# The first pair's scores and softmax ahead of the first weight group's conversion

## Chip, core and metric

The kernel runs on one NeuronCore of a Trainium2 chip. The metric is the device time of one execution in microseconds (us). The engines are TensorE (PE for matmuls, PEld for its weight loads), VectorE (DVE), ScalarE (ACT), GpSimd (POOL) and SyncE (SP, which here only issues DMAs).

## What is computed

Three stages run one after the other on 2304 tokens (4 batches of 576), all in float32:

```python
scores = q @ k^T / 8            # 4 batches, 8 heads, 576 tokens, head size 64
attn   = softmax(mask(scores))  # causal by blocks of 64 tokens
x      = attn @ v               # heads side by side: 2304 x 512
x = (sigmoid(x @ w_gate) * (x @ w_val)) @ w_out          # 512 -> 1536 -> 512
p = probs / sum(probs)
out = sum over 4 experts e:  p[:, e] * (relu(x @ w1[e]) @ w2[e])   # 512 -> 1024 -> 512
```

The weights of the middle stage arrive as 64-bit floats and are turned into 32-bit ones on the chip.

## The kernel before

**Precision.** A float32 product is made of three matmuls: each operand is split into a high part and the rest (`split_sb`: ACT or POOL writes the high part, DVE or POOL the rest). Sums of weight blocks and of activations save some of the products.

**Attention.** `attn_items` writes down a queue of steps for all 16 pairs of heads (4 batches of 4 pairs). A pair's scores are cut into tiles of 128 query rows, t = 0 to 4. A step `s_mm` makes a tile's scores on PE (line 350 for batch 0), then DVE masks (380), takes the row maximum (381, or 411 and 413 for the last tile, t4) and ACT the exponential (383, 416). Three steps later `p_tr` transposes the tile on PE (459, 479) and ACT copies it out (446, tiles pTa and pTb). `pv_both` multiplies with v (119, tile obank), makes the inverse sums (491 to 510) and scales (541). `prep_tr` transposes the next pair's q and k (230) with copies on ACT (238). The copies and the exponentials share ACT; the transposes of all steps share two PSUM banks (tbank). `loads` and `load_v` put a pair's DMAs on SP.

**Conversion.** `conv_items(f)` has twelve steps for one of twelve weight groups of the middle stage: `raw(0)` and `raw(1)` issue the two DMAs of 512 KB (647); `f64(0)` and `f64(1)` turn them into float32 (ACT 614, DVE 615 and 616); four `sums` on POOL (662) and four `part` steps split the results (ACT 131, DVE and POOL 129 and 133), and store them in DRAM (670, tile w1d) for later passes. There are three raw buffers, so the fourth raw DMA waits until the first buffer has been read by its last `sums`.

**Order.** Every step of the attention queue has a cost and so a place: its batch, plus the share of the batch's cost that lies ahead of it. `attn_to(A00)` first emits all steps with a place under 0.12 (items 0 to 21 of the queue). The rest of the queue up to place 1.05 (A1[0]) is then merged evenly with the conversion of the first five groups (NC0). After that come the first matmuls of the middle stage (L1: tiles c, weights wa, wb, wc, wd; it begins with group 4, whose parts stay in SBUF) and its inputs (`x1_prep`, tile xc), which need the four pairs of batch 0. Later steps of batches 1 to 3 and the conversion of groups 5 to 11 are mixed into L1.

**What the emitted order means.** It is a priority. The planner (`schedule_with_timeline_sim`) runs its own model of the engines and gives each engine's instructions the order in which they came up there; each engine then works through its list strictly in that order. `pinned(fn)` (102) ties each DVE, ACT and POOL instruction that `fn` emits behind the instruction emitted just before it on the same engine, in order alone, without a semaphore. Before the change only steps of the last middle pass use it (331).

Of the kernel before, what the change touches and what calls it, by code (L numbers as in the profile page):

```python
# [18 lines left out]
NC0 = 5  # L19
FIRST = (4, 0, 5, 1, 6, 2, 7, 3, 8, 9, 10, 11)  # L20
A00 = 0.12
A1 = [1.05, 2.3, 4, 4, 4]
PACE1 = 0.9
GB = 4
# [19 lines left out]
def _merge(a, b, pace=1.0):  # L44

    ta = sum(c for c, _ in a) or 1.0
    tb = sum(c for c, _ in b) or 1.0
    i = j = 0
    ca = cb = 0.0
    while i < len(a) or j < len(b):  # L50
        if j >= len(b) or (i < len(a) and pace * ca / ta <= cb / tb):
            c, fn = a[i]
            i += 1
            ca += c
        else:
            c, fn = b[j]
            j += 1
            cb += c
        fn()
# [3 lines left out]
def attention_moe_moe_kernel(  # L63
# [21 lines left out]
    NF = DFF // P  # L85
# [16 lines left out]
    def pinned(fn):  # L102

        def run_in_order():
            done = nc.cur_bb.bb.instructions
            n = len(done)
            fn()
            for i in range(n, len(done)):
                e = done[i].engine
                if e in (mybir.EngineType.DVE, mybir.EngineType.Activation, mybir.EngineType.Pool):  # L110
                    prev = next((x for x in reversed(done[:i]) if x.engine == e), None)
                    if prev is not None:
                        tc.add_manual_dep(done[i], prev.name, NOSYNC, reason="in the order given")

        return run_in_order
# [8 lines left out]
    def split_sb(hi, lo, src, eng_hi="v", eng_lo="v"):  # L124

        if eng_hi == "v":
            nc.vector.tensor_copy(out=hi, in_=src)
        elif eng_hi == "p":
            nc.gpsimd.tensor_scalar(out=hi, in0=src, scalar1=1.0, scalar2=1.0, op0=ALU.mult, op1=ALU.mult)
        else:  # L130
            nc.scalar.activation(out=hi, in_=src, func=AF.Copy)  # L131
        e = nc.vector if eng_lo == "v" else nc.gpsimd
        e.tensor_tensor(out=lo, in0=src, in1=hi.bitcast(F32), op=ALU.subtract)
# [474 lines left out]
    def from_f64(bits, out=None):  # L608

        lo, hi = bits[:, :, 0], bits[:, :, 1]
        f = lo if out is None else out.bitcast(I32)
        nc.scalar.activation(out=hi.bitcast(F32), in_=hi.bitcast(F32), func=AF.Prelu, scale=2.0 ** -112, alpha=2.0 ** 32)
        nc.vector.tensor_scalar(out=f, in0=lo, scalar1=29, scalar2=None, op0=ALU.logical_shift_right)
        nc.vector.scalar_tensor_tensor(  # L616
            out=f, in0=hi, scalar=3, in1=f, op0=ALU.logical_shift_left, op1=ALU.bitwise_or)
        return f.bitcast(F32)
# [15 lines left out]
    def w1_tile(k):  # L634
        n = 1 if k == "d" else 2
        return moe1.tile([P, 2, n, QF], F32R, tag="wd" if k == "d" else "wg", name=f"w{k}", bufs=2 if k == "d" else 6)

    def w1_at(f, k):
        return wc_d[f][:, WAT[k][0] * QF:WAT[k][1] * QF].rearrange("p (h n f) -> p h n f", h=2, f=QF)

    def conv_items(f):

        d = {}

        def raw(gv):
            t = d["raw", gv] = conv.tile([P, NKT, P, 2], I32, tag="raw", name="raw", bufs=3)
            nc.sync.dma_start(
                out=t.rearrange("p c f t -> p c (f t)"),
                in_=(w_gate, w_val)[gv].bitcast(I32)[:, 2 * f * P:2 * (f + 1) * P].rearrange("(c p) f -> p c f", p=P))

        def f64(gv):
            d[gv] = from_f64(d["raw", gv].rearrange("p c f t -> p (c f) t"))

        def b(k, a):
            return d[a][:, k * QF:(k + 1) * QF]

        def sums(n):
            if n == 0:
                d["t"] = conv.tile([P, 4, QF], F32, tag="wt", name="wt")
            t = d["t"]  # L660
            x, y = [(b(0, 1), b(0, 0)), (b(1, 1), t[:, 0]), (b(1, 1), b(0, 1)), (b(1, 0), t[:, 1])][n]
            nc.gpsimd.tensor_tensor(out=t[:, n], in0=x, in1=y, op=ALU.subtract)

        def part(k):
            t = w1_tile(k)
            src = dict(a=lambda: d[0], b=lambda: d["t"][:, 0:2].rearrange("p n f -> p (n f)"),
                       c=lambda: d["t"][:, 2:4].rearrange("p n f -> p (n f)"), d=lambda: b(1, 1))[k]()
            split_sb(t[:, 0].rearrange("p n f -> p (n f)"), t[:, 1].rearrange("p n f -> p (n f)"), src,
                     "p" if k in "bc" else "a", "v" if k == "a" else "p")
            nc.sync.dma_start(out=w1_at(f, k), in_=t.bitcast(F32))  # L670
            if f >= NC0 - 1:
                wg[f, k] = t

        r = [lambda: raw(0), lambda: raw(1), lambda: f64(0), lambda: f64(1), lambda: sums(0), lambda: part("a"),
             lambda: sums(1), lambda: part("b"), lambda: sums(2), lambda: sums(3), lambda: part("c"), lambda: part("d")]
        return [(1.0, x) for x in r]
# [229 lines left out]
    def run(lst):  # L906
        for _, fn in lst:
            fn()

    if True:  # L910
# [380 lines left out]
        def attn_next():  # L1291
            queue[pos[0]][3]()
            pos[0] += 1
            if pos[0] == len(queue):
                pt2.release()
                attn.release()

        def attn_to(target):
            while pos[0] < len(queue) and place[pos[0]] < target:
                attn_next()  # L1300

        attn_to(A00)
        a0 = [(queue[i][2], attn_next) for i in range(pos[0], len(queue)) if place[i] < A1[0]]
        cs = [conv_items(f) for f in range(NF)]
        _merge(a0, sum(cs[:NC0], []), 1.0)
        x_items = x1_prep(0)
        prev = []
        for p in range(NP1):
            at, total = 0.0, NF * 7 * 6 * C1 + NF * 2 * NKT * 3 * C1
            for f0 in range(0, NF, 2):  # L1310
# [39 lines left out]
                if f0 == NF - 2 and p == 0:  # L1350
                    x_items = x1_prep(p + 1)
                    n = len(items)
# [5 lines left out]
                for c, fn in both:  # L1358
                    attn_to(A1[p] + (A1[p + 1] - A1[p]) * min(1.0, at / total / PACE1))
                    fn()  # L1360
# [11 lines left out]
        for p in range(NPASS):  # L1372
            for q0 in range(0, NQ, 2):
                last = p == NPASS - 1 and q0 == NQ - 2
                items = l1_items(p, q0) + l1_items(p, q0 + 1)
                if (p, q0) == (0, 0):
                    m = len(items) // 2
                    items = [items[m * (c == "B") + "1526743".index(x)] for c, x in
                             ("A1", "A2", "A5", "B1", "A6", "B2", "A7", "B6", "B5", "A4", "B7", "A3", "B4", "B3")]
                side = []  # L1380
# [15 lines left out]
                n = len(items)  # L1396
# [48 lines left out]
```

## Time and profile before

| | |
|---|---|
| median of 3 runs | 1411.94 us (1411.53 to 1413.97) |
| profiled execution | 1413.05 us, span of its instructions 1411.3 us |
| PE busy | 1372.7 us (97% of the span) |
| DVE, ACT, POOL busy | 986.3, 777.6, 481.5 us |
| mean granted TensorE clock | 0.993 of 2.4 GHz |

In the profile's rows a time is in us from the start of the span, a mean in ns. A line of the timeline gives the start, the duration, the engine, the line of the kernel, the operation, the tile written and read, and in brackets how long the engine stood idle before and what ended that.

### The profile page before, as it was taken

The page shows a single profiled execution, that of the slowest core. Times are in us where ns is not written, and L with a number is a line of the kernel's source. Part 1 is how long each engine was busy: PE and PEld are TensorE (multiplying, and loading weights), DVE is VectorE, ACT ScalarE, POOL GpSimd, SP SyncE. Part 2 cuts the span into 40 slices and gives each one's busy share as a digit, 9 for nine tenths or more (in the row PEclk, how much of TensorE's full clock was granted, in tenths as well). Part 3 has the DMA queues.
Part 4 walks back from the last instruction along what each step waited for, and adds up shares of the span by engine and source line. Part 5 has one row for each costly group of instructions (what it writes and reads, how often), then busy time and mean ns, then how long its engine had stood idle before and what let it go on. Part 6 is the DMA issues. An engine that isn't in the chain of part 4 may idle for free.

```text
span 1411.3 us, 26204 instructions
## 1 busy us (share of the span) xinstructions
PE 1372.7 (97%) x9212; PEld 1267.3 (90%) x9212; DVE 986.3 (70%) x2103; ACT 777.6 (55%) x1926; POOL 481.5 (34%) x502
## 2 busy tenths in 40 slices
PE   6899999999999999999999999999999999999998
PEld 3467787889988999999999999989999999999998
DVE  6877689976776445466777666757766787766766
ACT  5888788888876333343445444544444454443442
POOL 4753346301122200022576556533222342322322
PEclk8999999999999999999999999999999999999999
DMA  7999677886657877998799888886666777676754
GB/s 224 299 285 294 214 237 249 267 238 201 194 165 226 298 262 268 319 341 299 273 340 350 298 301 305 288 301 232 232 251 241 258 259 283 245 270 229 275 206 157
DMA packets 210803, 369.57 MB, mean 262 GB/s; under 512 B 74736, under 2 KB 137200, under 8 KB 204528
## 3 DMA queue, kind: packets, MB, share of 16 engines
q1 hardware_dynamic: 209584, 367.62, 77.2%
q8 instruction: 74, 1.21, 0.3%
q14 instruction: 57, 0.47, 0.1%
q10 hardware_dynamic: 1088, 0.26, 0.1%
HBM read 267.82 MB, written 100.01 MB: 261 GB/s over the span
## 4 chain that ended last, share of the span: by engine, by line
PE 86%; DVE 4%; DMA 4%; ACT 3%; issue 1%; SPq 1%; POOL 1%; DVEq 0%; ACTq 0%; POOLq 0%
PE c L119 38%; PE o L119 26%; PE lo L119 7%; PE s L119 4%; PE obank L119 3%; PE t L119 3%; PE tbank L459 2%; DMA raw<-in_moe_w_val_dram 1%; PE s L350 1%; PE tbank L230 1%; PE tbank L479 1%; DVE raw L616 1%; DMA w1g<-w1d 1%; DVE nm L381 0%; ACT pt L383 0%
## 5 line engine op out<-in xcount | busy, mean ns | idle before, releaser
L119 PE MATMUL c<-xc,w1g 128*128 128x384 f32 x1920 | 384.6, 338 | 1.5 <-DMA w1g<-w1d 1.2
L119 PEld LDWEIGHTS c<-xc,w1g 128*128 128x128 f32 x1920 | 330.5, 188 | 7.7 <-DVE hb L1073 1.4
L119 PE MATMUL o<-w2s,hb 128*128 128x256 f32 x1728 | 243.5, 282 | 1.1 <-DVE acc L1222 1.1
L119 PEld LDWEIGHTS o<-w2s,hb 128*128 128x128 f32 x1728 | 231.8, 189 | 2.0 <-DVE acc L1222 1.7
L1222 DVE SCALAR_TENSOR_TENSOR acc<-o,pr_t,acc 128x256 f32<-128x256 f32 x264 | 123.4, 479 | 57.9 <-PE o L119 55.8
L1082 POOL TENSOR_TENSOR hs<-hf 128x384 f32<-128x384 f32 x64 | 64.0, 1022 | 287.5 <-ACT hf L1090 256.4
L119 PE MATMUL lo<-g,wo 128*128 128x288 f32 x888 | 150.8, 301 | 5.0 <-DVE x L895 3.0
L119 PE MATMUL o<-w,hb 128*128 128x512 f32 x576 | 142.8, 391 | 0.0
L119 PEld LDWEIGHTS lo<-g,wo 128*128 128x128 f32 x888 | 126.4, 188 | 11.0 <-DVE x L895 5.1
L1090 ACT ACTIVATE hf<-c 128x384 f32<-128x384 f32 x128 | 65.7, 513 | 115.1 <-DVE c L1127 57.8
L119 PEld LDWEIGHTS o<-w,hb 128*128 128x128 f32 x576 | 107.2, 188 | 18.5 <-DVE acc L1166 0.2
L1127 DVE TENSOR_TENSOR c<-c,snap 128x384 f32<-128x384 f32 x144 | 77.8, 552 | 56.0 <-PE c L119 38.4
L1120 ACT ACTIVATE snap<-c 128x384 f32<-128x384 f32 x144 | 65.7, 484 | 87.1 <-PE c L119 86.8
L1071 ACT ACTIVATE hb<-hs 128x384 fp32r<-128x384 f32 x128 | 63.3, 518 | 64.4 <-POOL hs L1082 64.2
L1073 DVE TENSOR_TENSOR hb<-hs,hb 128x384 fp32r<-128x384 f32 x128 | 87.2, 696 | 5.5 <-ACT hb L1071 5.2
L895 DVE TENSOR_TENSOR x<-lo,x 128x288 f32<-128x288 f32 x124 | 55.7, 453 | 45.7 <-PE lo L119 44.9
L119 PE MATMUL c<-xc,wa 128*128 128x288 f32 x504 | 83.9, 300 | 1.8 <-ACT xc L131 1.6
L383 ACT ACTIVATE pt<-s,nm 128x128 f32<-128x128 f32 (+3 forms) x128 | 67.5, 529 | 17.9 <-DVE nm L381 10.7
L119 PEld LDWEIGHTS c<-xc,wa 128*128 128x128 f32 x504 | 71.8, 189 | 4.2 <-ACT xc L131 2.2
L119 PE MATMUL c<-xc,wc 128*128 128x288 f32 x432 | 70.8, 298 | 0.4 <-ACT snap L819 0.4
L819 ACT ACTIVATE snap<-c 128x288 f32<-128x288 f32 x108 | 44.4, 411 | 41.4 <-PE c L119 41.0
L459 PE MATMUL tbank<-ident,pt 128*128 128x128 f32 x320 | 53.6, 282 | 12.5 <-ACT pTa L446 7.7
(180 smaller groups left out, 2707.1 us busy)
## 6 DMA issues: line engine op xcount, KB each, us to landing
w1g<-w1d SPq DMA_DIRECT2D x96, 512.0 KB, 5.3
w2s<-w2d SPq DMA_DIRECT2D x48, 1024.0 KB, 6.2
w1d<-w1g SPq DMA_DIRECT2D x48, 512.0 KB, 4.9
wa<-w1d SPq DMA_DIRECT2D x40, 512.0 KB, 5.0
wb<-w1d SPq DMA_DIRECT2D x40, 512.0 KB, 5.1
wc<-w1d SPq DMA_DIRECT2D x40, 512.0 KB, 4.3
wo<-wod SPq DMA_DIRECT2D x36, 512.0 KB, 5.8
wr<-in_moe_w_dram SPq DMA_DIRECT2D x32, 512.0 KB, 5.4
```

What stands on the lines that cost most here:

```text
L119: ins = nc.tensor.matmul(out=out, lhsT=lhsT, rhs=rhs, start=start, stop=stop, skip_group_check=skip)
L383: ins = nc.scalar.activation(out=pt[:, x * nk:(x + 1) * nk], in_=sp[:, x - x0], func=AF.Exp, bias=nm[:, j0 + x:j0 + x + 1], scale=1.0, acc ...
L459: nc.tensor.transpose(out=tbank[:, x * P:(x + 1) * P], in_=pt[:, x * P:(x + 1) * P], identity=ident)
L819: nc.scalar.activation(out=t, in_=d["c1"][:, :TH1], func=AF.Copy)
L895: nc.vector.tensor_tensor(out=x2[t, dm], in0=ps, in1=x2[t, dm], op=ALU.add)
L1071: nc.scalar.activation(out=t[:, 0], in_=src, func=AF.Copy if low is None else AF.Relu)
L1073: nc.vector.tensor_tensor(out=t[:, 1], in0=src, in1=t[:, 0].bitcast(F32), op=ALU.subtract)
L1082: nc.gpsimd.tensor_tensor(out=o, in0=x, in1=y, op=op)
L1090: nc.scalar.activation(out=hf[q, blk], in_=c, func=AF.Relu)
L1120: nc.scalar.activation(out=t, in_=d["c1"][:, :TH], func=AF.Copy)
L1127: nc.vector.tensor_tensor(out=c, in0=d[tag][:, :TH], in1=d[n], op=ALU.add)
L1222: nc.vector.scalar_tensor_tensor(out=o, in0=ps, scalar=pr, in1=o, op0=ALU.mult, op1=ALU.add)
```

## The change

```diff
+A01 = 0.25
...
         attn_to(A00)
+        cs = [conv_items(f) for f in range(NF)]
+        run(cs[0][:2])
+        attn_to(A01)
+        cs[0] = [(c, pinned(fn) if n < 2 else fn) for n, (c, fn) in enumerate(cs[0][2:])]
         a0 = [(queue[i][2], attn_next) for i in range(pos[0], len(queue)) if place[i] < A1[0]]
-        cs = [conv_items(f) for f in range(NF)]
         _merge(a0, sum(cs[:NC0], []), 1.0)
```

The two raw DMAs of group 0 are emitted right behind item 21. Then items 22 to 38 of the attention queue follow (places 0.124 to 0.240): all that is left of the first pair's scores and softmax with the transposes of its tiles, its first product with v, the keys of the second pair, the second pair's tiles t0 to t2, and the loads of the third pair. The other ten steps of group 0 come after them. `f64(0)` and `f64(1)` are pinned: their DVE and ACT instructions stand behind the last one emitted there. The 58 conversion steps that remain are merged with the attention steps from place 0.251 to 1.05.

## Rows read from the trace of the kernel before

**Rows 1.** Busy time, share and instructions of each engine.
```profile
PE 1372.7 (97%) x9212; PEld 1267.3 (90%) x9212; DVE 986.3 (70%) x2103; ACT 777.6 (55%) x1926; POOL 481.5 (34%) x502
```

**Rows 2.** Busy us (instructions) by stretch: stretch, length, engines, granted clock, DMA share, GB/s.
```profile
16.90:37.30 20.40, 12.41 (x63) 7.12 (x63) 19.00 (x42) 15.50 (x45) 15.94 (x17) 0.67 0.90 278
37.30:97.00 59.70, 52.04 (x347) 31.03 (x345) 49.35 (x135) 48.09 (x151) 38.23 (x43) 1.00 0.94 291
97.00:160.00 63.00, 62.29 (x436) 48.95 (x437) 47.45 (x120) 54.44 (x161) 25.00 (x26) 1.00 0.81 259
```

**Rows 3.** Timeline of PE around its longest stop.
```profile
16.76 0.38 PE L230 MATMUL tbank<-ident,qn 128*128 128x128 f32 x2
24.03 0.90 PE L459 MATMUL tbank<-ident,pt 128*128 128x128 f32 x3 [6.89 <-ACT pTa L446]
```

**Rows 4.** Timeline of ACT from 14 us to 37 us.
```profile
14.02 0.22 ACT L383 ACTIVATION_READ_ACCUMULATOR pt<-s,nm 128x1 f32 x1
16.93 0.69 ACT L614 ACTIVATE raw<-raw 128x512 f32<-128x512 f32 x1 [2.69 <-DMA raw<-in_moe_w_gate_dram]
...
21.20 0.50 ACT L416 ACTIVATE pt<-s,nm 128x288 f32<-128x288 f32 x1 [0.93 <-DVE nm L413]
...
23.38 0.59 ACT L446 ACTIVATE pTa<-tbank 128x512 f32<-128x512 f32 x1
...
36.68 0.60 ACT L446 ACTIVATE pTb<-tbank 128x512 f32<-128x512 f32 x1
```

**Rows 5.** Timeline of DVE: a wait for raw data, a long step, the second pair's t2.
```profile
16.93 0.43 DVE L615 TENSOR_SCALAR raw<-raw 128x512 int32<-128x512 int32 x1 [3.66 <-DMA raw<-in_moe_w_gate_dram]
17.27 0.45 DVE L411 TENSOR_REDUCE nm<-s 128x1 f32<-128x288 f32 x1
...
27.78 1.49 DVE L615 TENSOR_SCALAR raw<-raw 128x512 int32<-128x512 int32 x1
...
34.75 0.56 DVE L381 TENSOR_REDUCE nm<-s 128x1 f32<-128x384 f32 x1
```

**Rows 6.** Instructions on the raw tiles: busy us by stretch (DVE, ACT, POOL).
```profile
14.30:37.30 23.00, 10.27 (x13) 6.18 (x10) 8.79 (x10) 0.70 0.92 287
```

**Rows 7.** Short stretches: as rows 2.
```profile
8.00:12.00 4.00, 3.73 (x15) 1.94 (x16) 2.39 (x12) 2.20 (x9) 0.00 (x0) 1.00 0.69 155
12.00:14.00 2.00, 2.00 (x11) 0.86 (x9) 1.23 (x4) 1.54 (x5) 0.00 (x0) 1.00 0.94 152
...
17.20:20.00 2.80, 0.00 (x0) 0.00 (x0) 2.74 (x7) 1.81 (x4) 0.12 (x1) 0.88 1.06 209
20.00:22.00 2.00, 0.00 (x0) 0.00 (x0) 1.91 (x4) 1.07 (x4) 2.00 (x3) 0.50 0.99 349
```

**Rows 8.** The raw tiles: ns shortest/median/longest, first and last start.
```profile
L615 DVE TENSOR_SCALAR raw<-raw x36: 412/424/1491, 16.9 to 252.7; 128x512 int32<-128x512 int32 x36
L616 DVE SCALAR_TENSOR_TENSOR raw<-raw x36: 660/692/1659, 17.6 to 253.3; 128x512 int32<-128x512 int32 x36
...
L133 DVE TENSOR_TENSOR wa<-raw,wa x12: 666/683/1466, 19.7 to 239.5; 128x512 fp32r<-128x512 f32 x12
```

**Rows 9.** Timeline of SP's queue: third pair's loads, raw DMAs, group 1's return.
```profile
13.05 1.14 SPq L204 DMA_DIRECT2D qn<-in_q_dram  x2
...
16.40 1.62 SPq L204 DMA_DIRECT2D kn<-in_k_dram  x2
18.07 0.51 SPq L647 DMA_DIRECT2D raw<-in_moe_w_gate_dram  x1
...
104.80 0.32 SPq L681 DMA_DIRECT2D wa<-w1d  x1
```

**Rows 10.** Timeline of POOL: the last conversion step of group 4.
```profile
73.34 1.28 POOL L133 TENSOR_TENSOR wc<-wt,wc 128x512 fp32r<-128x512 f32 x1
```

**Rows 11.** Timeline of DVE: the fourth pair's last scaling.
```profile
89.11 0.49 DVE L541 TENSOR_TENSOR x<-obank,xr 128x320 f32<-128x320 f32 x1 [0.71 <-PE obank L119]
```

**Rows 12.** Timeline of PE: first products with group 4's wc and group 1's wa.
```profile
97.26 1.02 PE L119 MATMUL c<-xc,wc 128*128 128x288 f32 x6 [0.41 <-ACT snap L819]
...
130.64 1.84 PE L119 MATMUL c<-xc,wa 128*128 128x288 f32 x12
```

**Rows 13.** DMA issues between 100 and 140 us: count, KB, us to landing.
```profile
wa<-w1d SPq DMA_DIRECT2D x2, 512.0 KB, 5.9
```

## The prediction

> **What bounds the kernel now.** I read the page's totals first: PE is busy for 97% of the span [rows 1], so a gain has to come from the 38.6 us in which it is not, or from work that PE does slowly. The table of stretches shows where: from 16.9 to 37.3 us PE is busy for 12.41 of 20.40 us at a mean clock of 0.67, from 37.3 to 97 us for 52.04 of 59.70, and from 97 to 160 us for 62.29 of 63.00 [rows 2]. From 97 us on PE itself is the limit. Ahead of it the limit is the feeding of PE: the fourth pair's last scaling comes at 89.11 us [rows 11], and only behind it can the last inputs of L1 be made, while group 4's conversion, which L1 also needs, had its last POOL step at 73.34 us and is first wanted in its late part at 97.26 us [rows 10, 12]. So attention is late and conversion early, by 97.26 - 74.62 = 22.6 us. From 37.3 to 97 us DVE is busy for 83% and ACT for 81% [rows 2]: each is near its limit, and they hand work to each other.
>
> The timelines show what attention loses. PE stops for 6.89 us until 24.03 and waits for the copy pTa [rows 3]. ACT started that copy at 23.38, though the transposes had long been finished: its list puts steps of groups 0 and 1 and the exponentials of tile t4 ahead of it, and those wait for a row maximum [rows 4]. DVE in turn stood for 3.66 us until 16.93 in front of L615, the first step on the raw data, with the maximum of t4 queued behind it [rows 5]. ACT stood 2.69 us at the same data [rows 4].
>
> **The change part by part.** *Moved ahead.* Items 22 to 38 end with the copy of the first pair's last tile, which ACT ended at 36.68 + 0.60 = 37.28 us [rows 4]. ACT's earlier work ends at 14.24 [rows 4]. Between them ACT is busy for 15.50 us [rows 2], 6.18 of them on raw tiles in ten instructions [rows 6]; 9.32 us are attention's. At best ACT runs these without a gap but the 0.93 us for the maximum of t4 [rows 4]: 14.24 + 9.32 + 0.93 = 24.5. At worst it runs them at the share at which attention ran alone from 8 to 14 us, (2.20 + 1.54) / 6.00 = 62% [rows 7]: 14.24 + 15.0 = 29.2. I take the middle, 26.9, since three pair steps overlap here and not two. The lead of attention is then 37.3 - 26.9 = 10.4 us, with ends of 8.1 and 12.8. The stop of 6.89 us goes; what is late next on ACT is the pair of t3 exponentials, and then the tbank copies one behind another.
>
> *Moved behind.* `f64(0)` starts at about 26.9 instead of 16.93, 10 us later (7.6 to 12.3). Its DVE and ACT instructions, two of ACT and four of DVE with those of `f64(1)`, are tied to the end of item 38 on each engine; behind them stand the splits of group 0, and the fourth tiles of the second pair. POOL's steps and the stores are not tied but need these results. The work displaced is 10.27 us of DVE in 13 instructions and 6.18 of ACT in ten [rows 6].
>
> *DMAs.* The raw DMAs of group 0 keep their place. The third pair's loads, which move past group 0's stores, were already issued from 13.05 on, ahead of the third raw DMA at 18.07 [rows 9], so nothing changes in SP's order there; that third DMA has a free buffer and should go at the same time. From the fourth on, raw DMAs and stores follow group 0 by some 10 us. Two slacks cover this. Group 4 would end at 74.62 + 10 = 84.6 and is wanted at 97.26. Group 1's wa comes back by a DMA issued at 104.80 that lands 5.9 us later, and is first used at 130.64 [rows 9, 12, 13]: 19.9 us of slack. I cost the delay of conversion and of DMAs at nothing; if the cover were gone it would cost the part of 10 us beyond these.
>
> *Payback.* What was pushed behind has to be done before or beside pairs two to four. If all of it comes on attention's path, the lead shrinks by DVE's 10.27 us to 10.4 - 10.27 = 0.1. If all of it fits into the 59.70 - 49.35 = 10.35 us in which DVE is idle from 37.3 to 97 [rows 2], the whole 10.4 stays. Since DVE and ACT are over 80% busy there, most idle time is a wait inside a chain that other work can't use; I stay near the first end and take a third of the way: 0.1 + 10.3 / 3 = 3.5 us.
>
> How long is the displaced work really? L615, L616 and the split of wa have medians of 424, 692 and 683 ns, but longest cases of 1491, 1659 and 1466 [rows 8], and one of the long ones ran while POOL converted [rows 5]. At the medians, 5 x 0.424 + 5 x 0.692 + 3 x 0.683 = 7.6 us instead of 10.27. The Trainium skill, "SBUF — State Buffer", section "Who interferes with whom", says that a VectorE instruction with two SBUF inputs, or in a mode using both ports, fully blocks behind a GpSimd instruction; the longest rows agree. By that rule the change removes no blocking, it moves POOL's share of group 0 beside later pairs, and the sum would be the one above; with 7.6 it would be 10.4 - 7.6 + (a third of 7.6) = 5.3.
>
> *PE's clock.* In the stretch without matmuls the granted clock goes from 0.88 to 0.50, 1.2 of 2.4 GHz [rows 7]. The loss lies in the stretch that the first part already replaces, so I add nothing for it. The Trainium skill, "TensorE: Matmul & The Clock Gate", section "What's actually happening", says the throttled state is the default and activity releases it. That speaks against a full gain if PE is only lightly used by attention alone; from 8 to 12 us, where it was, the row shows 1.00 [rows 7].
>
> **Sum.** The profiled execution took 1413.05 us, 1.75 of them around its span of 1411.3. 1413.05 - 3.5 = 1409.5. The median of the runs shown is 1.1 us lower, 1411.94, so the median after is forecast at 1408.4 us, 0.25% faster. L1 would reach its full pace near 93.5 us, and I expect the work behind it, PE being the limit, to follow at the same distance.
>
> **The rivals.**
> *The lead stays nearly whole.* If conversion lags into its 22.6 us of slack and attention keeps running ahead, about 8 of the 10.4 us remain: 1404. For it: DVE and ACT idle time of 10.35 and 11.6 us from 37.3 to 97 [rows 2]. Against it: the merge after item 38 gives each attention step more conversion than before (58 steps in 0.80 of a batch, 1.38% each, against 60 in 0.93, 1.54% each), which spends the lead by design.
> *The lead is spent.* DVE pays back all of its 10.27 us, or the planner's order of the later pairs comes out much as now, because only DVE and ACT of two steps are tied: 0.1 us, 1411.8. For it: DVE is the busiest engine, 19.00 of 20.40 us and then 83% [rows 2].
> *DVE falls behind, slower.* Attention alone takes until 29.2, the lead is 8.1, and the payback 10.27: 2.2 us lost. On top, DVE's tie ends with the second pair's t2, whose last maximum now ends at 35.31 [rows 5], and ACT's with the copy that ends at 37.28 [rows 4]; L616 needs ACT's result, so DVE may stand up to 2.0 us with the maxima of the second pair behind it. Together 2 to 4 us, at 3 in all 1415. It decides from the point where the copy of item 38 ends later than 37.28 - 10.27 = 27.0 us and DVE has no idle time to use.
>
> **How the numbers follow.** This kernel's runs tell 0.2% (2.8 us) from no change. The forecast's own case, 1405 to 1411, has 0.48, of which 0.40 lies below 1409.1; the lead nearly whole 0.13; the lead spent 0.21; DVE behind 0.18. Faster by over 0.2% is 0.40 + 0.13 = 0.53, within 0.2% is 0.08 + 0.21 = 0.29, slower 0.18. The range goes from 1402.5, the lead kept with 1.5 us more of it than in the first rival, to 1415, the middle of the slower case; about 0.15 is left out.
>
> **What would show it.** PE's stop at 17 us gone and the clock at 1.00 from 16.9 to 37.3 us; the first L615 near 27 us instead of 16.93, with no wait for raw data in front; the first pair's last copy near 27; group 4's wc near 84; the fourth pair's last scaling at 85 to 86 instead of 89.11, and PE full from about 93.5. The prediction is wrong if the last scaling is not earlier although the stop is gone (the lead is spent), if DVE is over 90% busy from 27 to 90 us and the scaling is later, or if PE, full from 93.5, loses the time again between 97 and 260 us.

## The result, and the profile after

The changed kernel takes 1422.82 us (median of 6 runs, 1419.98 to 1425.03), the kernel before 1411.74 in the same session (6 runs, 1409.65 to 1413.97): a ratio of 1.0074 with a 95% interval of 1.0063 to 1.0086, so 9 to 12 us slower. The forecast was 1408.4 with a range to 1415; it was wrong in sign and the range missed.

The totals of the profile after answer to [rows 1]: no engine has more to do, only the span is 11.4 us longer (1422.7 against 1411.3). PE idles 49.6 us instead of 38.6.

```profile
PE 1373.1 (97%) x9212; PEld 1264.9 (89%) x9212; DVE 988.7 (69%) x2103; ACT 778.8 (55%) x1926; POOL 482.1 (34%) x502
```

Where PE idles shows in the stretches of the kernel after, in the columns of [rows 2]:

```profile
16.90:37.30 20.40, 13.78 (x75) 7.83 (x77) 8.70 (x30) 11.82 (x38) 0.00 (x0) 0.75 0.29 70
37.30:97.00 59.70, 47.58 (x322) 28.16 (x318) 53.05 (x133) 49.47 (x152) 45.43 (x49) 1.00 0.88 269
97.00:160.00 63.00, 60.45 (x407) 46.35 (x408) 45.16 (x111) 49.85 (x143) 27.17 (x28) 0.97 0.89 298
160.00:300.00 140.00, 130.60 (x923) 111.43 (x924) 124.18 (x298) 114.00 (x312) 63.70 (x60) 1.00 0.80 253
```

and one stretch of the kernel before that stands nowhere yet:

```profile
160.00:300.00 140.00, 134.76 (x963) 116.48 (x961) 121.47 (x305) 117.13 (x323) 53.22 (x53) 1.00 0.78 250
```

PE's busy time falls by 4.46 us from 37.3 to 97, by 1.84 from 97 to 160 and by 4.16 from 160 to 300: 10.5 of the 11.0 us. In the first stretch, where the gain was to arise, PE gains 1.4 us, and it loses as much ahead of it: up to 37.3 us PE is busy for 24.10 us after and 24.08 before. Look in that stretch at the last columns too: DVE does 8.70 us of work instead of 19.00, POOL none instead of 15.94, and the DMA engines are busy for 0.29 of the time instead of 0.90.

PE's stop is still there, and longer, in PE's timeline after (the row that answers to [rows 3]); ACT's, DVE's and SP's say why:

```profile
23.22 0.90 PE L460 MATMUL tbank<-ident,pt 128*128 128x128 f32 x3 [7.81 <-ACT pTa L447]
```
```profile
22.01 0.68 ACT L615 ACTIVATE raw<-raw 128x512 f32<-128x512 f32 x1 [4.70 <-DMA raw<-in_moe_w_gate_dram]
22.59 0.58 ACT L447 ACTIVATE pTa<-tbank 128x512 f32<-128x512 f32 x1
...
34.52 0.60 ACT L447 ACTIVATE pTb<-tbank 128x512 f32<-128x512 f32 x1
...
38.27 0.74 ACT L132 ACTIVATE wa<-raw 128x512 fp32r<-128x512 f32 x1
...
83.65 0.67 ACT L132 ACTIVATE wa<-raw 128x512 fp32r<-128x512 f32 x1
```
```profile
17.72 0.51 SPq L648 DMA_DIRECT2D raw<-in_moe_w_gate_dram  x1
18.32 1.00 SPq L205 DMA_DIRECT2D qn<-in_q_dram  x2
38.03 0.37 SPq L205 DMA_DIRECT2D vh<-in_v_dram  x1
```

Line numbers are one higher than before. The step at 22.01 isn't group 0's, which is tied: it is the first step of group 1, whose raw DMA is issued at 17.72 behind the third pair's loads. Nothing ties it, so the planner put it into the room that group 0 left, ahead of the copy pTa. The first pair's last copy ends at 34.52 + 0.60 = 35.12 us, 2.2 earlier than before [rows 4], not 10.4.

Behind 18.32 SP issues no DMA for 19.7 us. What stands next in its list is the third pair's load of v, which waits for the first pair's product with v; in the kernel before that load comes at 40.51, behind four more raw DMAs and the stores of groups 0 and 1. SP's wait after (us in all, times, longest), and the row before:

```profile
SPq L205 <- PE obank L120: 18.6, 1, 18.6
```
```profile
40.51 0.38 SPq L204 DMA_DIRECT2D vh<-in_v_dram  x1
```

The fourth raw DMA could hardly have gone earlier either: it needs a buffer that POOL's sums set free, and POOL's first sums come at 39.13 us.

What came late is conversion. ACT's copy into wa starts at 38.27 for group 0 and at 83.65 for group 4 (the first and the fifth such row); before, at 18.98 and 63.43:

```profile
18.98 0.65 ACT L131 ACTIVATE wa<-raw 128x512 fp32r<-128x512 f32 x1
...
63.43 0.70 ACT L131 ACTIVATE wa<-raw 128x512 fp32r<-128x512 f32 x1 [1.04 <-DVE raw L616]
```

19.3 us late at group 0 and 20.2 at group 4: nothing is made up. POOL's last step for group 4, at 73.34 before [rows 10], comes at 101.07, 27.7 later. PE's timeline before, then after, shows the price. The first products of L1 take group 4's wa, and before they stand among attention's matmuls:

```profile
73.86 1.03 PE L119 MATMUL c<-xc,wa 128*128 128x288 f32 x6
75.77 1.03 PE L119 MATMUL c<-xc,wa 128*128 128x288 f32 x3
81.16 0.40 PE L119 MATMUL c<-xc,wb 128*128 128x288 f32 x1
```
```profile
86.50 0.81 PE L120 MATMUL c<-xc,wa 128*128 128x288 f32 x4
...
97.27 1.07 PE L120 MATMUL c<-xc,wb 128*128 128x288 f32 x4 [0.75 <-POOL wb L130]
...
103.74 1.03 PE L120 MATMUL c<-xc,wc 128*128 128x288 f32 x6
...
140.61 0.96 PE L120 MATMUL c<-xc,wa 128*128 128x288 f32 x6
```

Group 4's wa is first used 12.6 us later, wb 16.1, wc 6.5, and group 1's wa 10.0 [rows 12]. The matmuls on L1's tile c show what PE loses of L1 from 37.3 to 97 us (before, then after; the columns are PE, PEld, DVE and ACT, clock, DMA share, GB/s):

```profile
37.30:97.00 59.70, 5.48 (x24) 3.53 (x24) 0.46 (x1) 0.68 (x2) 1.00 0.94 291
```
```profile
37.30:97.00 59.70, 2.38 (x12) 1.69 (x12) 0.44 (x1) 0.40 (x1) 1.00 0.88 269
```

Twelve of 24 are gone from there, 3.1 of the 4.46 us. Attention itself is not late: the fourth pair's last scaling is at 87.20 us, 1.9 earlier than [rows 11]:

```profile
87.20 0.49 DVE L542 TENSOR_TENSOR x<-obank,xr 128x320 f32<-128x320 f32 x1
```

### The profile page after: what moved, and what is told of

Read it like the earlier page. It is cut to its first block, busy times and chain, and to the rows that moved or that the text cites. A ratio compares the mean times of both kernels' runs of the same rounds, so it can differ in the third digit from the quotient of the medians.

```text
span 1422.7 us, 26191 instructions
## 1 busy us (share of the span) xinstructions
PE 1373.1 (97%) x9212; PEld 1264.9 (89%) x9212; DVE 988.7 (69%) x2103; ACT 778.8 (55%) x1926; POOL 482.1 (34%) x502
## 4 chain that ended last, share of the span: by engine, by line
PE 81%; DVE 5%; ACT 5%; DMA 5%; issue 2%; POOL 1%; SPq 0%; ACTq 0%; DVEq 0%; POOLq 0%
PE c L120 36%; PE o L120 25%; PE lo L120 6%; PE s L120 4%; PE obank L120 3%; PE t L120 3%; PE tbank L460 2%; PE s L351 1%; ACT pt L384 1%; DMA xr<-xd1b 1%; DVE xc L134 1%; DVE nm L382 1%; PE tbank L231 1%; DMA w1g<-w1d 1%; DMA raw<-in_moe_w_out_dram 1%
## 5 line engine op out<-in xcount | busy, mean ns | idle before, releaser
L120 PE MATMUL lo<-g,wo 128*128 128x288 f32 x888 | 147.7, 299 | 3.5 <-DVE x L896 3.5
L120 PEld LDWEIGHTS o<-w,hb 128*128 128x128 f32 x576 | 107.2, 188 | 18.6 <-DVE acc L1167 0.3
L120 PEld LDWEIGHTS c<-xc,wc 128*128 128x128 f32 x432 | 60.6, 188 | 7.9 <-ACT snap L820 4.7
```

The lines of the kernel that those rows point to most:

```text
L120: ins = nc.tensor.matmul(out=out, lhsT=lhsT, rhs=rhs, start=start, stop=stop, skip_group_check=skip)
```

## The experiments

In each a ratio is to the kernel before, run beside it. The first theory is *late conversion*: L1's first groups come late, and PE loses the L1 work that filled attention's gaps. Its first rival is *the step put ahead*: group 1's raw step and the stop of 7.81 us are the loss. A second one, named any reshuffle or a new order in the expectations, is that whatever order the planner makes anew is worse than the one before. (In the rows of e23 line numbers are two higher than before, in those of the other runs one.)

**e1_pin_next, e2_no_pin.** e1 ties group 1's two steps too; e2 takes the ties out and leaves the order of the program.

```diff
+        cs[1] = [(c, pinned(fn) if n in (2, 3) else fn) for n, (c, fn) in enumerate(cs[1])]   # e1
-        cs[0] = [(c, pinned(fn) if n < 2 else fn) for n, (c, fn) in enumerate(cs[0][2:])]
+        cs[0] = cs[0][2:]                                                                     # e2
```

> The changed kernel with group 1's two f64 steps pinned as group 0's are, so that none of them is put ahead. Late conversion (L1 waits for group 4, whose conversion ended 27.8 us later): PE's stop of 7.8 us goes and the first pair's last copy comes at 27 to 30 us, but group 4's last split still ends at 95 us or later, and the time stays at 1416 to 1423 us. Step put ahead (the stop in front of group 1's raw data is the loss): 1412 us or less.

> The changed kernel without the ties: the raw DMAs and attention steps are emitted early as in the change, and group 0's f64 steps are left to the planner. If the ties alone make the difference: 1412 us, as before, with the first conversion at 16.9 us. If the emitted order does: 1420 us or more.

e1: 1421.68 us, 1.0058 (1.0038 to 1.0078). Its stop is gone (largest wait of PE from 14 to 40 us: 2.45), and attention runs ahead as forecast; ACT's row of the first pair's last copy, and DVE's of the fourth pair's last scaling:

```profile
28.10 0.60 ACT L447 ACTIVATE pTb<-tbank 128x512 f32<-128x512 f32 x1
```
```profile
87.44 0.49 DVE L542 TENSOR_TENSOR x<-obank,xr 128x320 f32<-128x320 f32 x1
```

A lead of 8.6 us at the first, of 1.7 at the second, and still 8 us slower. So the step put ahead falls. e2: 1412.67 us, 0.9998 (0.9989 to 1.0007), and its lists of PE, DVE, ACT and POOL are those of the kernel before, instruction for instruction: the planner undoes the new place of the items, and six tied instructions make all of the difference.

**e3_pins_only, e9_pins_both, e6_a017.** The ties placed earlier: behind item 21 with group 0 alone (e3, without `attn_to(A01)`) or with group 1 too (e9), and at `A01 = 0.17` (e6).

> The ties alone: attention steps emitted ahead only up to item 21 as before the change, group 0's two f64 steps pinned there. Group 1's first step still comes ahead of them and waits for its data until about 22 us, so PE's stop stays, but group 0 converts some 10 us earlier than in the changed kernel. Late conversion: group 4 ends at 80 to 90 us, inside the slack, 1411 to 1415 us. Step put ahead: the stop costs as much as in the changed kernel, 1419 to 1423 us.

> Ties at item 21 for groups 0 and 1: no step waits for raw data ahead of the first pair's softmax, and group 0 converts from about 19 us. Both theories: no stop, conversion late by 2 to 4 us, 1407 to 1412 us. If it is slower than 1414 us, both miss something.

> The changed kernel with the tie a third of the way: items up to place 0.17 of the batch ahead of group 0's conversion instead of 0.25. Late conversion: the conversion chain is delayed by less, group 4's stores near 90 us instead of 102, so 1414 to 1418. The step put ahead: a group's raw data is still waited for ahead of the copies of the transposes, so a stop of 5 us or more near 20 us and 1419 to 1424. Any reshuffle costs: 1419 to 1424 too, but without that stop.

e3: 1429.95, 1.0105 (1.0078 to 1.0133); e9: 1418.61, 1.0038 (1.0026 to 1.0051); e6: 1419.78, 1.0044 (1.0030 to 1.0057). None fitted what late conversion expected. e3 and e9 are slower than any theory said; of e9 the expectation itself said that above 1414 us both miss something. e6 came out as the step put ahead had it, with a stop of 6.59 us and 1419.78, and with group 4 late by 16.8. But in e6 and e3 attention is late, not conversion alone: the fourth pair's last scaling is at 93.44 in e6 and at 100.55 in e3, 89.11 before. In e3 PE waits 6.4 us twice for copies and 4.7 once for DVE. A tie holds up what stands behind it on its engine. e9 is the run that late conversion explains least: group 4's wa copy is 5.4 us late, but its first product is 3.0 us earlier than before.

**e12_before_nc4, e11_after_nc4, e13_pin_nc4.** Four groups converted ahead of L1, group 3 first: the kernel before, the changed one, and e1.

```diff
-NC0 = 5
-FIRST = (4, 0, 5, 1, 6, 2, 7, 3, 8, 9, 10, 11)
+NC0 = 4
+FIRST = (3, 0, 4, 1, 5, 2, 6, 7, 8, 9, 10, 11)
```

> The kernel before with four weight groups converted ahead of L1 instead of five, and group 3 first in L1's order. It is the control of the next two. Late conversion: in the kernel before, conversion is not late, so nothing is gained, 1409 to 1415 us. Any reshuffle costs: the merge of attention and conversion changes from the start, so some 5 to 10 us more, 1417 to 1422.

> The changed kernel with four groups converted ahead of L1 and group 3 first. Group 3's stores come at 87.3 us in the changed kernel, group 4's at 102.4, and L1 wants the first group from about 97. Late conversion: the wait at L1's start goes, 1413 to 1417, at most 4 us above its control e12. The step put ahead (group 1's raw data waited for at 22 us, PE's stop of 7.81 us): the stop is untouched, so about 11 us above the control, 1420 to 1425. Any reshuffle costs: no relation to where L1 starts, 8 to 11 us above the control.

> As e11, with group 1's two steps tied as well (so that PE's stop at 17 to 30 us is gone, as in e1). Late conversion: the stop's 7 us are a gain once L1 no longer waits for a late group: 1405 to 1411, below its control e12. The step put ahead: the stop's going gains what it gained from after to e1, about 1 us below e11. Any reshuffle costs: as e11.

e12: 1421.94, 1.0057 (1.0039 to 1.0075); e11: 1423.16, 1.0067 (1.0052 to 1.0082); e13: 1419.54, 1.0041 (1.0028 to 1.0053). The levels missed, since the control itself lost 8 us. That loss is what the reshuffle theory had expected of it (1417 to 1422), and conversion isn't late in it: its third and fourth copies into wa start at 33.61 and 46.55 us, before at 34.42 and 47.22. The distances, though, are those of late conversion: the change costs 1.2 us here instead of 11, with its stop at 6.15 us, and with the stop gone (e13) it is 2.4 us below its control, where the reshuffle theory had e11 8 to 11 above. (The three intervals overlap.) With one group less before L1, the lateness delays little: the copy into group 3's wa starts at 72.60 in e11 and at 46.55 in e12, and L1's first product comes at 73.47 and 72.84.

**e14_kept, e17_late, e15_kept21, e16_a1.** Is it any new order by the planner that costs, as e12 suggests? In e14, e15 and e17 the order of PE, DVE, ACT and POOL is given, as a list of places in the program:

```diff
+        for a, b in zip(one, one[1:]):
+            tc.add_manual_dep(done[b], done[a].name, dep, reason="in the order given")
```

The list is the planner's for the kernel before, with the shifts that the expectations name. e16 has no list and no tie, but `A1 = [1.1, ...]`.

> The order of the instructions is given for PE, DVE, ACT and POOL: that of the kernel before, with the first pair's steps ahead of group 0's conversion as the change has them, conversion 10 us later at its start, this delay shrinking to 2 us at group 4's first split (64 to 66 us on the scale of the kernel before), PE's order untouched. Late conversion (PE's early L1 matmuls on group 4's wa, at 73.86 us in the kernel before and at 86.50 in the changed one, lose their place in attention's gaps): here they keep it, so 1404 to 1411 us. A new order of everything by the planner is what costs: also below 1412. If putting the first pair ahead is worth nothing in itself, 1411 to 1416; above 1416 both theories fall.

> As e14, but conversion stays 10 us late through group 4, and the L1 steps that need group 4 are put 6 us later in PE's, DVE's, ACT's and POOL's order, as the planner did with 12 us in the changed kernel; the attention steps stand as in e14. Late conversion: 5 to 12 us above e14, 1413 to 1421. A new order of everything: still the order of the kernel before within attention and within L1, so at most 3 us above e14, 1406 to 1413.

> The order of the kernel before is given for PE, DVE, ACT and POOL, with one change: the steps of groups 0 and 1 that stood ahead of items 17 to 21 on DVE (5 instructions) and ACT (5) stand right behind them. It is e9 with everything else kept. Late conversion: group 4 is not delayed, PE's stop of 6.89 us goes at least in part, 1406 to 1411. A new order of everything: 1406 to 1412 as well, where e9 had 1418.6. A raw step that only moves the stop elsewhere: 1411 to 1414.

> The kernel before without any tie and with the first constant of A1 at 1.1 instead of 1.05: four or five more attention items are shared out ahead of L1, which changes some 450 places of ACT's and PE's order from 40 us on and delays no conversion by much. Late conversion: 1409 to 1415. A new order of everything: 1416 to 1422.

e16: 1412.28, 0.9991 (0.9981 to 1.0002). It settles nothing: the 450 places of the expectation are not to be seen in its trace, where PE, DVE, ACT and POOL run the same operations on the same tiles in the same shapes and order as in the kernel before. It is a second run of that kernel, and shows the scatter: its copies into wa come 0.8 us earlier. So the reshuffle stays untested by it. e14: 1432.25, 1.0137 (1.0111 to 1.0162), above 1416, where by its expectation both theories fall. e17: 1443.14, 1.0213 (1.0197 to 1.0229), 10.9 us above e14, the distance that late conversion said but not its place: the fourth pair's last scaling is earlier than in e14 (93.26 against 107.52), and what PE loses lies from 97 to 160 us, where it is busy for 48.56 us against 58.65. e15: 1415.51 (ten runs, one of them at 2512.28), 1.0017 (1.0008 to 1.0027), nearest to the raw step that only moves the stop (1411 to 1414), and 1.5 us above its range.

e14 does for attention what was forecast: its first pair's last copy ends at 25.16 + 0.60 = 25.76 us (forecast 26.9). What follows shows in its stretches, and in its ACT and PE rows near 99 us:

```profile
20.00:30.00 10.00, 9.73 (x64) 5.01 (x62) 7.65 (x28) 8.88 (x32) 1.38 (x2) 1.00 0.26 72
...
90.00:100.00 10.00, 0.00 (x0) 0.00 (x0) 1.07 (x4) 1.31 (x5) 1.43 (x2) 0.51 1.01 358
```
```profile
99.14 0.69 ACT L615 ACTIVATE raw<-raw 128x512 f32<-128x512 f32 x1 [8.58 <-DMA raw<-in_moe_w_val_dram]
```
```profile
100.42 1.11 PE L460 MATMUL tbank<-ident,pt 128*128 128x128 f32 x4 [11.15 <-ACT pTb L447]
```

While attention runs alone, the DMA engines stand at 0.26: the three raw buffers hold data that waits for conversion, POOL's first sums come at 28.62 us, and SP stands in front of the third pair's load of v until 28.98. Later they are full (1.01), a raw DMA issued at 91.02 lands at 99, and a fixed order of ACT makes the copies wait behind it. e15 shows the same on a small scale: PE's first stop goes, and two others come, 5.55 us until 26.18, behind group 1's copy into wa, and 4.42 until 31.28, behind ACT's next raw step, on data whose DMA was issued at 26.36 instead of 23.30:

```profile
30.30 0.66 ACT L615 ACTIVATE raw<-raw 128x512 f32<-128x512 f32 x1 [4.18 <-DMA raw<-in_moe_w_val_dram]
```

That gives the third theory, *DMA*: from 14 to 97 us the DMA engines are busy for 0.93 of the time in the kernel before, so time that they lose may not be made up.

**e18_more_dma.** The kernel before in its own order, with 2 MB more to move:

```diff
+    for i in range(4):
+        more = dram.tile([NKT * P, 2 * P], I32, name=f"more{i}")
+        nc.sync.dma_start(out=more, in_=w_gate.bitcast(I32)[:, 2 * i * P:2 * (i + 1) * P])
```

> The kernel before, with its order given on all five engines, and four copies of 512 KB from DRAM to DRAM that nothing reads, put into SP's order behind the third raw DMA (18 us): at the 273 GB/s that the DMA engines moved from 14 to 20 us, 2.1 MB are 7.7 us of DMA time. No other work is added, and no step is moved. DMA theory (from 14 to 90 us the DMA engines are busy for 93% on average, so time that they lose is not made up, and conversion and L1's first steps come late by it): conversion's stores 5 to 8 us late through group 4, 1415 to 1420 us. Slack (the prediction's view: group 4 has 22.6 us): 1411 to 1414.

1416.67 us, 1.0023 (1.0013 to 1.0032), spans 1415.9 against 1411.3. That is at the lower edge of the DMA theory (1415 to 1420, with stores 5 to 8 us late; the kernel before had 1414.06 beside it): group 4's wa copy at 68.14 us, 4.7 late, and L1 with it; PE's first product with group 4's wa, and with group 0's:

```profile
78.54 1.03 PE L120 MATMUL c<-xc,wa 128*128 128x288 f32 x6
...
107.64 1.86 PE L120 MATMUL c<-xc,wa 128*128 128x288 f32 x12
```

Both are 4.7 us later than before (73.86 and 102.91), and the whole program 4.6 by the profiled spans, 3.2 by the ratio. But this is not a test of slack: 4.7 us is less than the 9.7 us between group 4's wa copy and its first product, too. In this run everything moves together, attention as well (its last scaling is at 93.81, 4.7 late), since the fixed order holds attention's ACT steps behind the late raw steps (PE waits 6.3 us for one, once). It shows that lost DMA time reaches the end of the program in a fixed order, not that it does so through L1's weights.

**e20_before_raw5, e19_after_raw5, e21_pin_raw5.** `bufs=5` for raw instead of 3 and 4 for wg instead of 6, in the kernel before, the changed one, and e1.

> The kernel before with five buffers for raw data instead of three, paid for by four wg buffers instead of six (there is no other room). Control of the next two. DMA theory: little raw data is waiting for a buffer, so no gain; fewer wg buffers may cost: 1411 to 1420. Slack: the same.

> The changed kernel with the same five and four buffers. Two more raw tiles, 1 MB or 3.8 us of DMA time, can be loaded while attention runs ahead, of the 14.5 us that DMA lost from 20 to 40 us (0.93 and 0.82 of 10 us each before, 0.23 and 0.07 after). DMA theory: the distance to its control e20 shrinks from 11 us to 4 to 8. Planner's order alone, or waits on ACT and DVE alone: it stays at 9 to 13.

> e1 (group 1's steps tied too) with the same five and four buffers. e1 lost 8.6 us of DMA time from 20 to 40 us and was 9 us above the kernel before. DMA theory: the distance to e20 shrinks to 2 to 6. The others: 7 to 11.

1436.62, 1443.42 and 1444.95 us; ratios 1.0155 (1.0128 to 1.0181), 1.0211 (1.0194 to 1.0228), 1.0215 (1.0199 to 1.0230). No theory had the control so high (1411 to 1420): the price of two wg buffers, 22 us, is larger than what was to be seen. e19 stands 6.8 us above its control, in the range of the DMA theory, e21 8.3, in that of the others. Inconclusive.

**e22_raw_act, e23_raw_act_late.** The other direction: time for group 0's raw DMAs where the DMA engines have some. Order as in the kernel before; the two DMAs go to ACT's queue, near 2.8 us (e22) and near 8 us (e23), instead of SP's at 11.87 and 12.42.

```diff
+NEARLY = 2
...
-            nc.sync.dma_start(
+            (nc.scalar if 2 * f + gv < NEARLY else nc.sync).dma_start(
```

> The kernel before with its order given, except that the two raw DMAs of group 0 are issued from ACT's queue right behind its four q loads (near 2.8 us) instead of from SP's at 11.87 and 12.42 us. From 4 to 12 us the DMA engines are busy for 0.30 to 0.72 of the time in the kernel before, so there is room. Conversion then needn't wait 3.66 us on DVE and 2.69 us on ACT for the raw data, and its buffers come free as much earlier. DMA theory: group 4's wa is split 3 to 4 us earlier (64.1 us before) and L1 starts as much earlier: 2 to 4 us below the kernel before. Slack theory: the stop of PE alone shortens, 0 to 1.5 us below. If the first pair's loads are slowed by the 1 MB beside them: up to 3 us above.

> As e22, with the two raw DMAs behind ACT's five copies of the first transposes (near 8.2 us), where most of the first pair's loads have landed. DMA theory: 2 to 4 us below the kernel before, as e22 but without slowing the first loads. Slack theory: 0 to 1.5 us below.

e22: 1412.15, 0.9993 (0.9983 to 1.0003). It slowed one of the first loads (PE waits 1.9 us for kn, which it doesn't before; its 3.7 for qn are 3.9 before), and group 4 comes 0.2 us later than before. e23: 1411.09, 0.9985 (0.9976 to 0.9994), the only version whose interval lies below the kernel before, by 1 to 3 us; e16, with that kernel's own order, came out at 0.9991, so little of it is sure. Its rows of DVE, of a stretch, and of ACT for group 4:

```profile
13.40 0.42 DVE L617 TENSOR_SCALAR raw<-raw 128x512 int32<-128x512 int32 x1
```
```profile
20.00:30.00 10.00, 5.07 (x23) 3.30 (x25) 5.70 (x13) 5.67 (x15) 6.46 (x8) 0.51 1.02 350
```
```profile
61.88 0.68 ACT L133 ACTIVATE wa<-raw 128x512 fp32r<-128x512 f32 x1 [1.01 <-DVE raw L618]
```

Conversion starts 3.5 us earlier than at 16.93 [rows 5]. PE's stop stays (7.5 us, once). By group 4, 1.5 us of the 3.5 are left, with the DMA engines at 1.02 from 20 to 30 us, and attention has moved by as much (its last scaling is at 87.55, 1.6 earlier). The time falls by 1.8, less than the DMA theory expected (2 to 4) and a little more than slack did (0 to 1.5).

The runs side by side, all from timelines and stretches (times in us):

| kernel | DMA share, 20 to 40 us | wa copy of group 0, of group 4 | first product, group 4 | fourth pair's last scaling | ratio |
|---|---|---|---|---|---|
| e23 | 0.93 | 15.75, 61.88 | 72.28 | 87.55 | 0.9985 |
| e16 | 0.89 | 18.10, 62.62 | 73.04 | 88.28 | 0.9991 |
| before | 0.87 | 18.98, 63.43 | 73.86 | 89.11 | 1 |
| e15 | 0.76 | 21.12, 67.60 | 78.00 | 93.25 | 1.0017 |
| e18 | 0.98 (its copies counted) | 18.66, 68.14 | 78.54 | 93.81 | 1.0023 |
| e9 | 0.71 | 20.56, 68.82 | 70.83 | 90.71 | 1.0038 |
| e6 | 0.29 | 32.70, 80.27 | 81.00 | 93.44 | 1.0044 |
| e1 | 0.44 | 31.85, 77.71 | 78.62 | 87.44 | 1.0058 |
| after | 0.15 | 38.27, 83.65 | 86.50 | 87.20 | 1.0074 |

No row makes up a delay of group 0 by group 4. In e23, e16, before, e15 and e18 the order is the same or nearly so, and group 4's copy, its first product and the last scaling move together, with 10.4 us from the start of the copy to the product. Conversion is late with attention early in e1 and the changed kernel alone. There, as in e6 and e9, the first product follows the end of the copy into wa (which takes 0.7 us) within 0.1 to 2.2 us: most of the slack is used up. e3, e14 and e17 lie outside, since attention or a raw step holds PE up in them.

## Why the prediction was wrong

*The step that failed* is the one that cost the delay of conversion, and of its DMAs, at nothing. It read group 4's slack from its last tile: wc, done at 74.62, wanted at 97.26 [rows 10, 12]. L1 starts with the first: wa, whose copy on ACT ends at 64.13, is wanted at 73.86. That is 9.7 us, not 22.6; the first row of PE with any tile of group 4 shows it. The runs showed in its place a group 4 that is 20.2 us late, twice those 9.7, with L1's first product 12.6 us late and half of L1's matmuls gone from the stretch up to 97 us.

*How late.* The step had conversion follow by 10 us. It follows by 19.3 at group 0, and POOL's last step of group 4 came at 101.07, not near 84. Two reasons. The first is shown by the timeline after and by e1: the lead was smaller, since group 1's untied step waited for raw data in front of the first pair. The second is that a delay is kept through group 4, which the table shows. That nothing changes in SP's order was wrong too: it held for the third pair's q and k, but its load of v moved ahead of four raw DMAs and stood 18.6 us in front of them; no run shows what that alone costs. The prediction's own row had the DMA engines at 0.94 from 37.3 to 97 us [rows 2], and it used that row for DVE and ACT alone. After, they stand at 0.15 from 20 to 40. e18 and e23 show that DMA time lost or won early arrives at L1 in a fixed order, with attention beside it. The Trainium skill, "Perfetto Trace Analysis", section "Identifying the Most-Contended Engine", says to judge DMA by the memory's utilization and not by busy time, as sixteen engines make the latter misleading. By busy time hardly any room was left here. Against the limit of about 358 GB/s for one core that "DMA: Bandwidth & Descriptors" of the Trainium skill gives under "Specifications", the 291 GB/s of [rows 2] would be 81%, an estimate. e18 found part of the room that this leaves (334 GB/s from 16.9 to 37.3 us, 278 before) and was still 4.7 us late, so neither column told it alone.

*The stop goes, first pair at 26.9.* Wrong in the changed kernel (7.81 us, 35.12), right where group 1 is held back too: 28.70 in e1 and 25.76 in e14, both inside 24.5 to 29.2. The clock from 16.9 to 37.3 us, forecast at 1.00, was 1.00 in e1 and 0.75 in the changed kernel. The working on ACT held; that nothing else would be put there did not. (The row from 8 to 12 us is no row of a lightly used PE: it has it busy for 3.73 of 4.00 us [rows 7].)

*Payback.* Forecast: 6.9 of a lead of 10.4 are paid back. e1: a lead of 8.6 becomes 1.7, so 6.9, the same by luck as far as these runs tell, since e1 is another order; in the changed kernel 2.2 becomes 1.9. It was worth nothing: with attention 1.7 to 1.9 us earlier at the fourth pair both kernels are slower.

*DVE's displaced work, 7.6 or 10.27.* DVE's total went from 986.3 [rows 1] to 988.7 us, and its longest steps on raw tiles are as long as before (1529, 1711 and 1573 ns), so the change removed no blocking between DVE and POOL, as the prediction had it by the Trainium skill, "SBUF — State Buffer", section "Who interferes with whom".

*The rivals.* None named late conversion. "DVE falls behind" had the sign and 1415, but DVE is busy for 53.05 of 59.70 us from 37.3 to 97 and attention is early. "The lead is spent", because only two steps are tied, had it that two ties leave the later order as it is; they don't (e2 against the changed kernel).

*What stays open.* Whether late conversion is the whole cause. That the delay reaches L1's products is shown by the rows; that it makes all of the 11 us is argued. The rival that the planner's new order costs by itself is not excluded: e12 lost 8 us with conversion on time, e16 didn't test it, and only the distances of e11 and e13 to e12 speak against it. Nor is it shown how the 11 us divide. Up to 160 us PE idles 6.3 us more, in the stretch in which L1's first groups are late. The 4.2 from 160 to 300 us go with groups 5 to 7, whose wa copies end 11 to 16 us late, but only 1.4 of them are matmuls on tile c (57.66 us against 59.06), and no run isolates them. Nor does one tell the DMA engines' lost time from the time that DVE, ACT and POOL lost beside it, from 16.9 to 37.3 us; e18 takes the first alone, but in a fixed order. And e9 has no explanation: its attention is 1.6 us late and its clock was 0.66 from 80 to 90 us and 0.83 from 50 to 60, where the kernel before has 1.00, but e1 had a clock of 0.83 too, from 50 to 60 and from 90 to 100.

## What to carry to other kernels

Before you cost a delay at nothing, look for the first instruction that reads *any* part of what is delayed, and read the DMA column of the stretch in which the delay is to be made up. A producer that runs ahead through few buffers is a pump: while it stands, its loads stand, and where the DMA engines were nearly full afterwards, as here (0.88 from 37.3 to 97 us), the delay arrived whole (19.3 us became 20.2). And where a planner orders the program, a tie on one step makes room that the next untied step of the same kind takes; tie the class or none.

## What the runs showed of the hardware

DMAs issued from another queue came earlier, not faster. SP took 0.5 to 0.7 us per DMA up to 13 us, with 18 of them ahead of group 0's two, so these waited in line until 11.87 us. From ACT's queue the first was issued at 7.55 and landed 5.4 us later, from SP's 5.0 us later, and the first step on its data starts at 13.40 instead of 16.93. The Trainium skill, "DMA: Bandwidth & Descriptors", section "Issuing engines are not separate DMA queues", says that a second issuing engine saves only time on the sequencer, usually small against the DMA itself. The trace agrees with the first half (5.4 us to land against 5.0); the second half holds for one DMA of 0.5 us, but here a line of 18 kept two back: issued 4.3 us earlier, they let the first step come 3.5 us earlier.

And 2 MB of copies that nothing reads, 18 us into the program, cost 3.2 us of 1412 (0.0013 to 0.0032 of the time) in a fixed order of all engines, though PE is busy for 97% of the span.
